# Rounding float64 weights with fewer VectorE instructions, and running the first tile's first two steps in parts

## The chip, the cores and the metric

One core of one Trainium2 chip. The metric is device time of one execution in microseconds (us). The kernel before takes 1192.2 us (median of 4 runs, 1190.4 to 1193.2).

Names: TensorE (PE in the profile) multiplies matrices, VectorE (DVE) and ScalarE (ACT) work elementwise, GpSimd (POOL) does the slow elementwise rest, and one queue (SPq) issues all the DMA requests of the program. The banks (bankA, mix and so on) are the pieces of memory that the matmuls write. A cold clock is a stretch in which the profile shows TensorE's granted clock at 0.50 of full speed.

## The reference, cut to what matters

```python
# B=8, H=8, S=576, D=64; x becomes (4608, 512); d_ff = 1536
scores = scale * q @ k.T                       # per batch and head
ret    = scores * gamma[h] ** (i - j)          # for i >= j, else 0
x      = (ret @ v) laid out as (B*S, H*D)
g      = x @ w_gate
out    = (silu(g) * (x @ w_val)) @ w_out       # w_* come as float64
```

## The kernel before

The attention runs in 32 "ticks" (batch and pair of heads). Each tick handles three stages of three neighbouring pairs: `values` of pair t-2, `scores` of pair t-1, `transposes` of pair t. The output is computed in nine tiles of 512 rows. The first tile is special: while it runs, the 18 blocks of weights (1 MB each, as 64-bit words) are loaded and turned into 32-bit floats by integer arithmetic. Later tiles use a scheme with fewer matmuls.

```python
def load_w(i):                     # three raw buffers; SP queue
    raw = rawp.tile([P, 1024], I64, tag="raw", bufs=RAWS)      # RAWS = 3
    nc.sync.dma_start(out=raw..., in_=src...)

def weight(i):                     # one block of weights
    nc.vector.tensor_scalar(out=ex, in0=hi, 20, 0x7FF, shift_right, and)
    nc.scalar.activation(out=ex, in_=ex, func=AF.Relu, bias=low, scale=float(1 << 23))
    nc.vector.tensor_scalar(out=man, in0=hi, 0xFFFFF, 0x100000, and, or)
    nc.vector.scalar_tensor_tensor(out=sig, in0=lo, 2.0 ** -32, in1=man, mult, add)
    nc.vector.scalar_tensor_tensor(out=ex, in0=hi, -(1 << 31), in1=ex, and, or)
    nc.vector.scalar_tensor_tensor(out=dst, in0=sig, 2.0 ** -20, in1=ex, mult, mult)
    load_w(the weight three further on)
...
def transposes(i):                 # of pair i
    ...; load(i + AHEAD)           # request the attention tiles of pair i + 2
    for hl in range(2):            # key scaling, on ScalarE
        nc.scalar.activation(out=kn[:, :, hl, :], in_=kn[:, :, hl, :], func=AF.Copy, scale=key[...])
...
def up(f):                         # one of 12 steps of the first tile
    ...16 matmuls into two banks...
    s = rawp.tile([P, TW], F32, tag="s", bufs=2)               # same pool as the raw weights
    nc.scalar.activation(out=s, in_=banks[0], func=AF.Silu)
    nc.vector.tensor_tensor(out=hs[:, f], in0=banks[1], in1=s, op=ALU.mult)
...
merge(ticks(0, 6), [weights 0, 1, 2])          # spread evenly, in program order
merge(ticks(6, 10), moe + four down groups)    # moe: 12 steps, 15 weights
first.close()                                  # the pool rawp is released here
up_ = tc.tile_pool(name="up", bufs=2)          # its tiles lie where rawp lay
xs[1] = combos_x(1)                            # sums for the second tile, VectorE
```

The program sets the order by hand: every engine runs its instructions in the order in which they are emitted.

## Time and profile before

| Part of the span | us | what bounds it |
|---|---|---|
| to 5 | 5 | first loads |
| 5 to 67.9 | 63 | loads, VectorE; the first two steps end at 67.9 |
| 67.9 to 208.9 | 141 | ten steps, four ticks, four down groups; TensorE with waits |
| 208.9 to 219.8 | 11 | the second tile's first two groups (3.5 us of matmuls) |
| 219.8 to 1190 | 970 | TensorE without idle time |

The prediction shows the lines it rests on. One more view: busy time by stretch of 30 us. The columns are stretch and length; busy us and number of instructions of PE, PEld (weight loads), DVE, ACT, POOL; granted TensorE clock; mean busy share of the 16 DMA engines (a value over 1 shows that it isn't exact); GB/s.

```profile
30.00:60.00 30.00, 23.38 (x223) 16.28 (x224) 24.87 (x44) 9.90 (x17) 0.00 (x0) 0.83 0.86 180
60.00:90.00 30.00, 30.00 (x133) 14.85 (x132) 25.23 (x36) 6.96 (x9) 3.87 (x2) 1.00 1.05 209
90.00:120.00 30.00, 21.68 (x110) 11.36 (x109) 28.06 (x38) 6.47 (x8) 1.26 (x1) 0.89 0.76 236
```

VectorE is at 24.9 to 28.1 of 30 us, and the DMA engines are nearly as full.

### The profile page before, as it was taken

The numbers are of one execution on the slowest core, as the hardware profiler recorded it, in microseconds if no ns is written. First come the engines' busy times: TensorE is split into PE (matmuls) and PEld (weight loads), VectorE is DVE, ScalarE is ACT, GpSimd is POOL, SyncE is SP. The second block draws the span as 40 slices with busy tenths as digits, with TensorE's granted clock in tenths as the row PEclk, the third lists the DMA queues.
The fourth block names the chain that finished last, engine by engine and source line by source line (L and its number), as shares of the span: only waits on it lengthen the run. The fifth ranks groups of instructions, "written<-read, shape, count | busy, mean of one in ns | idle before, by whom it ended". The sixth has DMA issues, their size and how long they took to land.

```text
span 1190.0 us, 16346 instructions
## 1 busy us (share of the span) xinstructions
PE 1149.8 (97%) x6660; PEld 945.7 (79%) x6660; DVE 519.3 (44%) x922; ACT 168.8 (14%) x324; POOL 425.8 (36%) x382
## 2 busy tenths in 40 slices
PE   5797999899999999999999999999999999999998
PEld 4543444688888888888888888888888888888887
DVE  3889940444335443444344444444343333333332
ACT  2322210111011110111011101110111001101110
POOL 0010100553433434444244325434344436345541
PEclk9898999899999999999999999999999999999999
DMA  9897610132212221222222221222000010000001
GB/s 233 182 212 226 205 34 32 22 66 40 40 36 45 53 49 47 40 40 39 66 49 39 40 57 42 55 40 48 28 1 1 1 36 1 1 18 18 1 0 36
DMA packets 228299, 65.96 MB, mean 55 GB/s; under 512 B 211584, under 2 KB 219776, under 8 KB 228224
## 3 DMA queue, kind: packets, MB, share of 16 engines
q1 hardware_dynamic: 228224, 64.92, 23.8%
q8 instruction: 52, 0.85, 0.3%
q14 instruction: 23, 0.19, 0.1%
HBM read 55.45 MB, written 9.44 MB: 55 GB/s over the span
## 4 chain that ended last, share of the span: by engine, by line
PE 89%; DVE 4%; SPq 3%; DMA 3%; issue 1%; ACT 0%; DVEq 0%; ACTq 0%
PE bankE L380 14%; PE bankC L380 14%; PE bankA L380 14%; PE bankB L380 7%; PE bankE L450 7%; PE bankC L450 7%; PE bankA L450 7%; PE bankB L450 3%; PE sc L264 2%; PE xo L286 2%; PE mix L270 1%; PE xo L294 1%; SPq L133 1%; PE bankA L338 1%; PE bankA L346 1%; PE bankE L338 1%
## 5 line engine op out<-in xcount | busy, mean ns | idle before, releaser
L380 PE MATMUL bankA<-x,w_up 128*128 128x256 f32 x768 | 182.0, 380 | 0.0
L424 POOL TENSOR_TENSOR hid<-c,ss 128x512 f32<-128x512 f32 x48 | 61.0, 1271 | 326.1 <-ACT ss L423 326.1
L380 PEld LDWEIGHTS bankA<-x,w_up 128*128 128x128 f32 x768 | 145.4, 190 | 20.4 <-issue 0.5
L380 PE MATMUL bankB<-t,s 128*128 128x256 f32 x384 | 92.6, 385 | 5.2 <-DVE t L369 5.2
L380 PE MATMUL bankE<-x,w_up 128*128 128x256 f32 x384 | 91.3, 381 | 0.0
L380 PE MATMUL bankE<-x,s 128*128 128x256 f32 x384 | 91.3, 381 | 0.0
L399 DVE TENSOR_TENSOR u<-bankB,u 128x512 f32<-128x512 f32 x48 | 33.2, 692 | 132.7 <-PE bankB L380 122.9
L380 PE MATMUL bankC<-t,s 128*128 128x256 f32 x384 | 91.1, 380 | 0.0
L380 PE MATMUL bankC<-t,w_up 128*128 128x256 f32 x384 | 90.7, 379 | 0.0
L380 PEld LDWEIGHTS bankB<-t,s 128*128 128x128 f32 x384 | 74.0, 193 | 15.8 <-POOL s L358 5.6
L450 PE MATMUL bankE<-w_dn,hid 128*128 128x256 f32 x384 | 86.1, 381 | 0.0
L450 PE MATMUL bankC<-t,hid 128*128 128x256 f32 x384 | 85.5, 379 | 0.0
L450 PE MATMUL bankA<-w_dn,hid 128*128 128x256 f32 x384 | 85.5, 379 | 0.0
L380 PEld LDWEIGHTS bankC<-t,s 128*128 128x128 f32 x384 | 73.4, 191 | 10.1
L380 PEld LDWEIGHTS bankC<-t,w_up 128*128 128x128 f32 x384 | 73.0, 190 | 9.9
L450 PEld LDWEIGHTS bankA<-w_dn,hid 128*128 128x128 f32 x384 | 73.0, 190 | 9.9
L450 PEld LDWEIGHTS bankC<-t,hid 128*128 128x128 f32 x384 | 73.0, 190 | 9.9
L380 PEld LDWEIGHTS bankE<-x,w_up 128*128 128x128 f32 x384 | 72.5, 190 | 10.0
L450 PEld LDWEIGHTS bankE<-w_dn,hid 128*128 128x128 f32 x384 | 72.5, 190 | 10.0
L380 PEld LDWEIGHTS bankE<-x,s 128*128 128x128 f32 x384 | 72.5, 190 | 10.0
L357 POOL TENSOR_TENSOR s<-w_up 128x512 f32<-128x512 f32 x48 | 61.4, 1279 | 51.4 <-DMA out_dram<-o 51.4
L415 ACT ACTIVATE s<-bankA 128x256 f32<-128x256 f32 x48 | 18.4, 383 | 353.0 <-PE bankA L380 353.0
(105 smaller groups left out, 1535.4 us busy)
## 6 DMA issues: line engine op xcount, KB each, us to landing
kn<-in_k_dram SPq DMA_DIRECT2D x64, 128.0 KB, 2.9
v<-in_v_dram SPq DMA_DIRECT2D x64, 128.0 KB, 3.0
qk<-in_q_dram SPq DMA_DIRECT2D x112, 72.0 KB, 2.5
qk<-in_k_dram SPq DMA_DIRECT2D x112, 72.0 KB, 2.6
raw<-in_moe_w_gate_dram SPq DMA_DIRECT2D x6, 1024.0 KB, 7.3
raw<-in_moe_w_val_dram SPq DMA_DIRECT2D x6, 1024.0 KB, 5.3
raw<-in_moe_w_out_dram SPq DMA_DIRECT2D x6, 1024.0 KB, 5.4
out_dram<-c SPq DMA_DIRECT2D x16, 256.0 KB, 2.2
```

Source lines behind the costliest of these rows:

```text
L133: nc.sync.dma_start(out=qk[a * SQ : (a + 1) * SQ, n], in_=src[b, 2 * p + a // 2, :, (a % 2) * SQ : (a % 2 + 1) * SQ].rearrange("(j t) d -> ...
L264: nc.tensor.matmul(sc[hl][:, ts(c, P)], kT[half[hl], ts(c, P)], qT[half[hl], ts(c, P)], start=True, stop=True)
L270: nc.tensor.matmul(z[half[hl], c], s["kn"][:, c, hl, :], s["v"][:, c, hl, :], start=True, stop=True)
L286: nc.tensor.matmul(xo[half[hl], ts(c, P)], s["v"][:, c, hl, :], ret[:, hl, ts(c, P)], start=(c == 0), stop=(c == 0), skip_group_check=True)
L294: nc.tensor.matmul(o[half[hl]], state[half[hl], c - 1, :], s["qT"][half[hl], c * P : c * P + w], start=False, stop=True, skip_group_check= ...
L338: nc.tensor.matmul(bank, w_up[:, u, gv, c // 2, c % 2, fb, :], x[:, c, :], start=(c == 0), stop=(c == HP - 1))
L357: nc.gpsimd.tensor_tensor(out=s2, in0=A(u, 1, 0), in1=A(u, 0, 0), op=ALU.subtract)
L380: nc.tensor.matmul(bank[:, gv * TH : (gv + 1) * TH], lhs(gv, c), rhs[:, c, :], start=(start and gv == 0 and c == 0), stop=(stop and c == 1 ...
L399: nc.vector.tensor_tensor(out=uu, in0=bankB, in1=uu, op=ALU.add)
L415: nc.scalar.activation(out=s, in_=bankA[:, 0:TH], func=AF.Silu)
L424: nc.gpsimd.tensor_tensor(out=hid[:, u, 1::2], in0=t["c"][:, :, 1], in1=s, op=ALU.mult)
L450: nc.tensor.matmul(bank[:, m * DH : (m + 1) * DH], lhs(u)[:, ts(m, P)], rhs(u), start=(start and u == 0 and m == 0), stop=(stop and u == N ...
```

## The change

The intent: VectorE's five instructions per weight become three, ScalarE splits the 64-bit words, TensorE is fed early by running steps 0 and 1 in parts as each quarter of `x` arrives, and the first tile's output buffers move out of the pool that is released. The diff, cut to its core:

```diff
+    io = ctx.enter_context(tc.tile_pool(name="io", bufs=2))
+    def split(i):
+        nc.scalar.activation(out=top, in_=high words as F32, func=AF.Copy, scale=2.0 ** -112)
+        nc.scalar.activation(out=ulp, in_=low words as U32, func=AF.Copy, scale=2.0 ** -29)
     def weight(i):
-        (five VectorE instructions and one ScalarE, above)
+        nc.vector.tensor_scalar(out=top, in0=top, scalar1=3, op0=ALU.logical_shift_left)
+        nc.vector.scalar_tensor_tensor(out=top, in0=hi, scalar=-(1 << 31), in1=top, and, or)
+        nc.vector.tensor_tensor(out=dst.bitcast(I32), in0=top, in1=ulp, op=ALU.add)
         load_w(order[k + RAWS])
+        split(order[k + 1])            # the next weight's split, right behind this weight
     load_w(0); load(1); load_w(1)
-    load_w(2)
 def transposes(i):
     load(i + AHEAD)
+    if i == 1: load_w(2)
-    key scaling of pair i on ScalarE
 def scores(i):
+    key scaling of pair i on ScalarE   # one tick later than before
-    s, o in rawp; ss in up_
+    s, o, ss in io
-    merge(ticks(0, done), [weights 0, 1, 2])
+    split(0)
+    for t in range(done):
+        tick(t)
+        if t in (1, 2, 3): weight(t - 1)
+        if 2 < t < 6: up(0 and 1, chunks 0 and 1 at t == 3, else chunk t - 2)
     moe: steps and weights, two weights ahead of step 2;
+    the last two weights both behind step 11
```

More of the change, by code (lines that the diff above doesn't have):

```diff
@@ L177 @@
     LEAD, RAWS = 3, 3
-    order = list(range(LEAD))
-    for f in range(2 * NU):
-        order += [LEAD + f] if LEAD + f < NUP else []
-        order += [NUP + f // 2] if f % 2 else []
+    behind = [[] for _ in range(2 * NU)]
+    for f in range(1, 2 * NU):
+        behind[f] += [LEAD + f] if LEAD + f < NUP else []
+        behind[f] += [NUP + (f - 3) // 2] if f % 2 and f > 1 else []
+    behind[1].insert(0, LEAD)
+    behind[-1].append(len(weights) - 1)
+    order = list(range(LEAD)) + sum(behind, [])
+    assert sorted(order) == list(range(len(weights)))
     first = ExitStack()
     rawp = first.enter_context(tc.tile_pool(name="rawp", bufs=1))
-    raws = {}
+    raws, parts = {}, {}
     def load_w(i):
@@ L190, in load_w @@
         raws[i] = raw.bitcast(I32).rearrange("p (n two) -> p n two", two=2)
-    def weight(i):
-        dst, bits = weights[i][1], raws.pop(i)
-        lo, hi = bits[:, :, 0].bitcast(U32), bits[:, :, 1]
-        ex = rawp.tile([P, 1024], I32, tag="ex", name="ex")
-        man = rawp.tile([P, 1024], I32, tag="man", name="man")
-        nc.vector.tensor_scalar(out=ex, in0=hi, scalar1=20, scalar2=0x7FF,
-                                op0=ALU.logical_shift_right, op1=ALU.bitwise_and)
-        nc.scalar.activation(out=ex, in_=ex, func=AF.Relu, bias=low, scale=float(1 << 23))
-        nc.vector.tensor_scalar(out=man, in0=hi, scalar1=0xFFFFF, scalar2=0x100000,
-                                op0=ALU.bitwise_and, op1=ALU.bitwise_or)
-        sig = man.bitcast(F32)
-        nc.vector.scalar_tensor_tensor(out=sig, in0=lo, scalar=2.0 ** -32, in1=man, op0=ALU.mult, op1=ALU.add)
-        nc.vector.scalar_tensor_tensor(out=ex, in0=hi, scalar=-(1 << 31), in1=ex,
-                                       op0=ALU.bitwise_and, op1=ALU.bitwise_or)
-        nc.vector.scalar_tensor_tensor(out=dst, in0=sig, scalar=2.0 ** -20, in1=ex.bitcast(F32),
-                                       op0=ALU.mult, op1=ALU.mult)
-        if order.index(i) + RAWS < len(order):
-            load_w(order[order.index(i) + RAWS])
@@ L213 @@
-    low = const.tile([P, 1], F32, name="low")
-    nc.gpsimd.memset(low, -896.0 * (1 << 23))
+    def split(i):
+        bits = raws[i]
+        top = rawp.tile([P, 1024], F32, tag="top", name="top", bufs=2)
+        nc.scalar.activation(out=top, in_=bits[:, :, 1].bitcast(F32), func=AF.Copy, scale=2.0 ** -112)
+        ulp = rawp.tile([P, 1024], I32, tag="ulp", name="ulp", bufs=2)
+        nc.scalar.activation(out=ulp, in_=bits[:, :, 0].bitcast(U32), func=AF.Copy, scale=2.0 ** -29)
+        parts[i] = top.bitcast(I32), ulp
@@ new lines, in weight @@
+    def weight(i):
+        dst, hi = weights[i][1], raws.pop(i)[:, :, 1]
+        top, ulp = parts.pop(i)
+        nc.vector.tensor_scalar(out=top, in0=top, scalar1=3, scalar2=None, op0=ALU.logical_shift_left)
+        nc.vector.scalar_tensor_tensor(out=top, in0=hi, scalar=-(1 << 31), in1=top,
+                                       op0=ALU.bitwise_and, op1=ALU.bitwise_or)
+        nc.vector.tensor_tensor(out=dst.bitcast(I32), in0=top, in1=ulp, op=ALU.add)
+        k = order.index(i)
+        if k + RAWS < len(order):
+            load_w(order[k + RAWS])
+        if k + 1 < len(order):
+            split(order[k + 1])
@@ L217 @@
         load(i)
-    for i in range(1, RAWS):
-        load_w(i)
+    load_w(1)
     kT = const.tile([P, S], F32, name="kT")
@@ L253, in transposes, with scores @@
             load(i + AHEAD)
+        if i == 1:
+            load_w(2)
+        st[i] = dict(qT=qT, kn=kn, v=vt, last=last)
+    def scores(i):
+        p, s = i % HP, st[i]
+        qT, kn = s["qT"], s["kn"]
         for hl in range(2):
@@ L256, in transposes @@
                                  scale=key[:, 2 * p + hl : 2 * p + hl + 1])
-        st[i] = dict(qT=qT, kn=kn, v=vt, last=last)
-    def scores(i):
-        p, s = i % HP, st[i]
-        qT = s["qT"]
         for c in range(NFULL):
@@ L269, in scores @@
             for hl in range(2):
-                nc.tensor.matmul(z[half[hl], c], s["kn"][:, c, hl, :], s["v"][:, c, hl, :], start=True, stop=True)
+                nc.tensor.matmul(z[half[hl], c], kn[:, c, hl, :], s["v"][:, c, hl, :], start=True, stop=True)
         for hl in range(2):
@@ L330, in plain, with up @@
         hs = hid.rearrange("p u b t -> p (u b t)").rearrange("p (f t) -> p f t", t=TW)
-        def up(f):
+        def up(f, chunks):
             u, fb = divmod(f, 2)
@@ L336, in up @@
             for gv, bank in enumerate(banks):
-                for c in range(HP):
+                for c in chunks:
                     nc.tensor.matmul(bank, w_up[:, u, gv, c // 2, c % 2, fb, :], x[:, c, :], start=(c == 0), stop=(c == HP - 1))
-            s = rawp.tile([P, TW], F32, tag="s", name="s", bufs=2)
-            nc.scalar.activation(out=s, in_=banks[0], func=AF.Silu)
-            nc.vector.tensor_tensor(out=hs[:, f], in0=banks[1], in1=s, op=ALU.mult)
+            if HP - 1 in chunks:
+                s = io.tile([P, TW], F32, tag="s", name="s")
+                nc.scalar.activation(out=s, in_=banks[0], func=AF.Silu)
+                nc.vector.tensor_tensor(out=hs[:, f], in0=banks[1], in1=s, op=ALU.mult)
         def down(i):
@@ L347, in down @@
                                  start=(f == 0), stop=(f == 2 * NU - 1))
-            o = rawp.tile([P, DM], F32, tag="s", name="o", bufs=2)
+            o = io.tile([P, DM], F32, tag="s", name="o")
             nc.scalar.copy(out=o, in_=bank)
             nc.sync.dma_start(out=out[n * TW + i * P : n * TW + (i + 1) * P, :], in_=o)
-        return [lambda f=f: up(f) for f in range(2 * NU)] + [lambda i=i: down(i) for i in range(TW // P)]
+        return up, down
     def combos_up(u):
@@ L421, in p4 @@
                                     in1=t["u"].rearrange("p g t -> p (g t)"), op=ALU.add)
-            s = up_.tile([P, 2, TH], F32, tag="ss", name="ss", bufs=1)
+            s = io.tile([P, 2, TH], F32, tag="s", name="ss")
             nc.scalar.activation(out=s, in_=t["c"][:, :, 0], func=AF.Silu)
@@ L510, in p2 @@
             mm(bankA, h(1), w(1, 0), False, True)
-            s = up_.tile([P, 2, DH], F32, tag="ss", name="ss", bufs=1)
+            s = io.tile([P, 2, DH], F32, tag="s", name="o")
             nc.scalar.copy(out=flat(s), in_=bankA)
@@ L547 @@
     done = needed(0)
-    merge(ticks(0, done), [lambda i=i: weight(i) for i in range(LEAD)])
-    steps = plain(0)
-    moe = []
-    for f in range(2 * NU):
-        moe += [lambda i=LEAD + f: weight(i)] if LEAD + f < NUP else []
-        moe.append(steps[f])
-        moe += [lambda u=f // 2: weight(NUP + u)] if f % 2 else []
-    merge(ticks(done, needed(1)), moe + steps[2 * NU :])
+    up, down_plain = plain(0)
+    split(0)
+    for t in range(done):
+        tick(t)
+        if t in (1, 2, 3):
+            weight(t - 1)
+        if t - 2 in range(HP) and t > 2:
+            for f in range(2):
+                up(f, range(2) if t == 3 else [t - 2])
+    moe = []
+    for f in range(1, 2 * NU):
+        moe += [lambda f=f: up(f, range(HP))] if f > 1 else []
+        moe += [lambda i=i: weight(i) for i in behind[f]]
+    merge(ticks(done, needed(1)), moe + [lambda i=i: down_plain(i) for i in range(TW // P)])
     done = needed(1)
```

## The prediction

> **What bounds the kernel now.** I read the page first: its busy shares, then its 40 slices.
>
> ```profile
> PE 1149.8 (97%) x6660; PEld 945.7 (79%) x6660; DVE 519.3 (44%) x922; ACT 168.8 (14%) x324; POOL 425.8 (36%) x382
> PE   5797999899999999999999999999999999999998
> DVE  3889940444335443444344444444343333333332
> ```
>
> TensorE bounds the whole, and from slice 8 (about 220 us) on it has no idle time to give. The change can only shorten the opening, the first tile; there VectorE is at 8 to 9 tenths in slices 1 to 4. So the question is how much TensorE idles before 220 us. The waits of TensorE in the first 330 us answer it (engine, line, whom it waited for: us, times, longest):
>
> ```profile
> PE mix L267 <- DVE x L309: 18.7, 5, 8.3
> PE bankA L244 <- DMA qk<-in_q_dram: 8.1, 2, 5.3
> PE bankB L380 <- DVE t L369: 5.2, 1, 5.2
> PE bankB L244 <- DMA kn<-in_k_dram: 2.1, 3, 1.0
> ```
>
> The 18.7 us are five waits for one small VectorE instruction that frees a PSUM bank. The timeline shows why it is late: it stands in VectorE's queue behind a weight conversion (start, duration, instruction):
>
> ```profile
> 161.02 0.69 DVE L341 TENSOR_TENSOR hid<-bankE,s 128x512 f32<-128x512 f32 x1 [6.18 <-PE bankE L338]
> 161.63 0.68 DVE L199 TENSOR_SCALAR ex<-raw 128x1024 int32<-128x1024 int32 x1
> ...
> 166.49 0.22 DVE L309 TENSOR_TENSOR x<-mix,tab 128x64 f32<-128x64 f32 x1
> ```
>
> The chain that ended last shows the 5.2 us at the end of the first tile:
>
> ```profile
> 209.19 0.59 ACT o L349
> 209.80 2.00 DMA out_dram<-o
> 211.92 0.70 DVE t L367
> 212.65 1.64 DVE x L368
> 214.32 1.64 DVE t L369
> 216.05 3.75 PE bankB L380 x8
> 219.80 2.04 PE bankC L380 x8
> ```
>
> The second tile's sums wait for the last store of the first tile, because their buffers lie where the released pool with `o` lay. Then the eight matmuls take 3.75 us; later groups of the same kind take 1.73.
>
> The conversion's cost by instruction (count, busy us, mean ns):
>
> ```profile
> L205 DVE SCALAR_TENSOR_TENSOR man<-raw,man 128x1024 f32<-128x1024 uint32 x18 | 22.2, 1232 | 0.6
> L206 DVE SCALAR_TENSOR_TENSOR ex<-raw,ex 128x1024 int32<-128x1024 int32 x18 | 21.9, 1217 | 0.6 <-ACT ex L201 0.6
> L202 DVE TENSOR_SCALAR man<-raw 128x1024 int32<-128x1024 int32 x18 | 13.4, 746 | 0.0
> L199 DVE TENSOR_SCALAR ex<-raw 128x1024 int32<-128x1024 int32 x18 | 12.7, 705 | 16.3 <-DMA raw<-in_moe_w_gate_dram 14.0 <-DMA raw<-in_moe_w_out_dram 1.5 <-DMA raw<-in_moe_w_val_dram 0.7
> L201 ACT ACTIVATE ex<-ex,low 128x1024 int32<-128x1024 int32 x18 | 20.7, 1150 | 77.4 <-DVE ex L199 77.4
> DMA to landing us min/median/max: 4.8/5.5/8.6
> ```
>
> The last line is for the raw weights, 1 MB each. The fifth conversion instruction (L208) has a mean of 1308 ns into `w_up`.
>
> **What the Trainium skill says.** "VectorE: DVE Perf Modes", the perf-mode tier table: an fp32 one-source operation from SBUF runs at two elements a cycle, a tensor_tensor at one. The trace agrees for these 32-bit words: about 0.7 us against 1.22 for 1024. The same page's Specifications say integer operands are converted to fp32 and exact only below 2^24; if so, the new integer addition rounds the weights a little, which costs no time; no run yet shows it. "ScalarE: Activation LUTs", What ACT_TABLE_LOAD costs: 186 ns + 0.833 ns an element with immediates, 93 more for a pointer operand. For 1024 that is 1132 ns with the bias of before (trace: 1150) and 1039 without. "TensorE: Matmul & The Clock Gate", Part 1: after about 3.4 us of idling the array runs at half rate for a similar time. The trace agrees: after a wait of 3.8 us at 50 us, eight matmuls into bankA took 6.06 us instead of 3.43.
>
> **The change part by part.**
> VectorE: five instructions become three. One shift (0.69), one sign merge (1.22), one add of two SBUF tensors (1.22): 3.13 us, against 0.69+0.69+1.23+1.22+1.23 = 5.06. 18 x 1.93 = 35 us less VectorE work.
> ScalarE: one activation of 1.15 becomes two of about 1.04, so 18 x 0.93 = 17 us more. It is 20 to 33% busy in the opening, so the load is harmless. The position isn't: each engine keeps program order, and the split of weight k+1 stands right after weight k. It then blocks whatever follows on ScalarE until that raw weight has landed. I see three places.
> (a) The first split precedes tick 0. Weight 0 landed at 14.0 us (the first VectorE instruction started then), so the copies of qT, which ran at 6.5, run at 16.0. TensorE's first scores move from 9.2 to about 17.3. Before, tick 1 then waited to 15.5 for its load anyhow, so tick 1 ends near 23.7 and little is lost against before.
> (b) Weight 2 is now requested behind the fourth attention load, which can't start before tick 1's transposes (23.7) and takes 6.8 us to issue. 23.7 + 6.8 + 5.5 = 36. Its split ends at 38, the key scaling of tick 3 at 39; TensorE is ready at 33.6. About 6 us idle, and a cold clock after.
> (c) Weight 6 is requested behind the load of tick 5 (14 issues, 7.6 us, after VectorE's transposes). Its split stands ahead of tick 6's key scaling: about 4 us idle.
>
> TensorE, traced forward by these durations: tick 2 ends at 30; tick 3 with (b) at 42; the first part of the two moved steps (8 half-banks, 6.9 us, 1.5 for the cold clock) at 50.5; tick 4 at 54.8; 3.4 us of parts, 58.2; tick 5 at 62.4; the last 3.4 us of parts, 65.8. Before, the same work (bankE of the second step) ended at 67.9. So moving the two steps, 13.7 us of matmuls, into the gaps gains about 2 us, because the new ScalarE waits take up the gaps.
> From there TensorE must run ten steps of two banks of 3.43, so 6.87 each, 68.7; four ticks of 4.1 (67.9 to 71.9 in the timeline), 16.4; four down groups of 10.3, 41.2; two groups of the second tile, 3.5: together 129.8.
> Gaps on top: waiting for weight 3 0.6; tick 6 0.9 + 4.3 and 1.5 cold; tick 7 0.8; tick 8 about 0; tick 9: weights 16 and 17 now both stand between the last product and the bank's release, 0.7 + 6.26 + 0.2 against 3.2 us of other TensorE work, 4.0, and 1.5 cold. Sum 13.6.
> The wait at the end of the tile goes: the output tiles now lie in a pool of their own, so the sums run during the down groups, 41 us earlier. That takes out 5.2 and the cold 2.0.
> So the second group of the second tile ends at 65.8 + 129.8 + 13.6 = 209.2 instead of 219.8: 10.6 us less, 1182. Of this 7.2 are the end of the tile, 2 the moved steps, the rest smaller waits behind shorter conversions. After 220 us nothing changes but one more buffer for `ss`, whose engine has slack.
>
> **The rivals.**
> First, a clean win: if no ScalarE wait appears, TensorE runs on from tick 2 at 23.7: 8 ticks of 4.1, 2 transposes of 1.8, 24 banks of 3.43, 41.2 and 3.5 give 32.8+3.6+82.3+41.2+3.5+23.7 = 187 instead of 219.8; 1160. For it: VectorE's 35 us are real work on a busy engine. Against: the program order on ScalarE, and the order of requests.
> Second, DMA becomes the bound. Its share was 0.91, 0.86 and 1.05 in the first three stretches of 30 us, and up to the last weight it moves some 31 MB at about 230 GB/s, 135 us. The last weights are needed near 150, so it just fits; but three raw buffers cover only two landings ahead, and each late one now also blocks Silu and key scaling. That would give back 5 to 10 us more: 1187 to 1192.
> Third, the tile's end alone matters and all else cancels: 1185.
>
> **Range and chances.** The step sum says 1182. Gaps of hand-traced queues can fall together, so I lean a little towards the win: 1180.5, with 1169 to 1189 as the range. Faster by over 2% needs under 1168.8, more than twice my gain and most of the clean win: 0.11. Slower by over 2% would need a new wait in the long part, which I see nowhere: 0.01.
>
> **What would show it.** Right: VectorE's conversion in three groups of about 0.69, 1.22, 1.22 us; ScalarE idle until 14 us for the first raw weight; TensorE's matmuls of `mix` from `kn` waiting for ScalarE in ticks 3 and 6; no wait of L369's kind before the second tile; the first down group starting near 164.5 instead of 167.7. Wrong: TensorE without waits from 24 us on (the clean win), Silu held by raw weights in many steps (DMA), a conversion over 4 us, or a change after the first tile.

## The result, and the profile after

The changed kernel takes 1184.07 us (median of 4 runs, 1183.73 to 1184.24), 0.9933 of the kernel before (95% interval 0.9916 to 0.995): 8 us less.

The page first: VectorE has 36 us less work (519.3 before), ScalarE 18 us more (168.8), and TensorE is as dense as before from slice 8 on.

```profile
PE 1145.0 (97%) x6660; PEld 942.2 (80%) x6660; DVE 483.5 (41%) x886; ACT 186.7 (16%) x342; POOL 422.7 (36%) x381
```

The new conversion, groups on VectorE and then on ScalarE (count, busy us, mean ns):

```profile
L215 DVE SCALAR_TENSOR_TENSOR top<-raw,top 128x1024 int32<-128x1024 int32 x18 | 22.1, 1225 | 0.6
L217 DVE CUSTOM_DVE_ANT_0 w_up<-top,ulp 128x2048 uint16<-128x2048 uint16 x12 | 14.7, 1225 | 0.8
L214 DVE TENSOR_SCALAR top<-top 128x1024 int32<-128x1024 int32 x18 | 12.3, 682 | 0.0
...
L203 ACT ACTIVATE top<-raw 128x1024 f32<-128x1024 f32 x18 | 20.7, 1148 | 48.3 <-DMA raw<-in_moe_w_gate_dram 27.9 <-DVE w_up L217 12.4 <-DMA raw<-in_moe_w_out_dram 5.0
```

The integer addition turns up as a custom instruction on 16-bit halves; it takes 1.225 us all the same. The last line is the one that matters: ScalarE stood 48.3 us idle at the head of a split, mostly for raw weights that had not landed.

Whom TensorE waited for, in the first 330 us (compare the list in the prediction):

```profile
PE mix L280 <- ACT kn L270: 11.3, 2, 6.0
PE sc L274 <- ACT kT L253: 8.1, 1, 8.1
PE mix L277 <- DVE x L319: 6.7, 4, 4.2
PE bankA L252 <- DMA qk<-in_q_dram: 5.2, 1, 5.2
...
```

The wait for the bank fell from 18.7 to 6.7 us, and the one of 5.2 us at the tile's end is gone. Two came: 11.3 us for the scaled keys, which is new, and 8.1 us for the first copies (0.5 before), both on ScalarE. The chain of waits shows how the larger one comes about:

```profile
73.97 5.47 DMA raw<-in_moe_w_gate_dram
79.52 1.12 ACT top L203
80.64 1.01 ACT ulp L205
82.09 1.51 PE mix L280 x16
83.60 5.28 PE bankC L348 x8
...
208.59 1.73 PE bankA L391 x8
210.32 1.73 PE bankB L391 x8
```

Weight 6 is requested at 74.0, although its raw buffer was free from 66.6: the 14 requests of the load of pair 7 stood ahead of it in the queue, from 66.2 to 73.9. It lands at 79.5, is split until 81.5, then the keys of tick 6 are scaled, and only then can TensorE go on. Then a cold clock stretches eight matmuls from 3.43 to 5.28 us (the mean granted clock of the stretch from 60 to 90 us is 0.89). At the end, the second tile's second group follows the first without a gap and ends at 212.05 (210.32 + 1.73) instead of 219.80. That difference, 7.75 us, is nearly the whole gain: the span is 8.0 us shorter. The second tile's sums now run during the down groups; the last of them on VectorE:

```profile
169.81 0.69 DVE L380 TENSOR_TENSOR t<-x 128x512 f32<-128x512 f32 x1
```

After the second group nothing changed: from the start of the third to the end are 970.4 us before and 970.1 after, so the second buffer for `ss`, which came with the new pool, is no rival.

### The profile page after: what moved, and what is told of

The parts are those of the page before. It is cut to its first block, busy times and chain, and to the rows that moved or that the text cites. A ratio compares the mean times of both kernels' runs of the same rounds, so it can differ in the third digit from the quotient of the medians.

```text
span 1182.0 us, 16354 instructions
## 1 busy us (share of the span) xinstructions
PE 1145.0 (97%) x6660; PEld 942.2 (80%) x6660; DVE 483.5 (41%) x886; ACT 186.7 (16%) x342; POOL 422.7 (36%) x381
## 4 chain that ended last, share of the span: by engine, by line
PE 95%; DMA 1%; DVE 1%; ACT 1%; SPq 1%; issue 1%; DVEq 0%; ACTq 0%
PE bankE L391 14%; PE bankA L391 14%; PE bankC L391 14%; PE bankE L461 7%; PE bankC L461 7%; PE bankB L391 7%; PE bankA L461 7%; PE bankB L461 4%; PE sc L274 3%; PE xo L296 2%; PE bankC L348 2%; PE mix L280 2%; PE bankB L348 2%; PE bankA L348 2%; PE xo L304 2%; PE bankE L348 1%
## 5 line engine op out<-in xcount | busy, mean ns | idle before, releaser
L461 PE MATMUL bankC<-t,hid 128*128 128x256 f32 x384 | 85.5, 379 | 0.0
L461 PE MATMUL bankA<-w_dn,hid 128*128 128x256 f32 x384 | 85.5, 379 | 0.0
```

What stands on the lines that cost most here:

```text
L461: nc.tensor.matmul(bank[:, m * DH : (m + 1) * DH], lhs(u)[:, ts(m, P)], rhs(u), start=(start and u == 0 and m == 0), stop=(stop and u == N ...
```

## The experiments

The theory to test: the gain is the end of the first tile; all else cancels, since ScalarE's stands at late weights take back what the shorter conversion gives. The rivals: the conversion itself pays; the parts pay; DMA is the bound. Twelve kernels ran, all with results that agree with the reference within its tolerance. Runs of one call shared a chip and its runs of the kernel before (median 1192.1, 1193.5, 1192.5 and 1192.8 us in the four calls), so runs of different calls are compared by their ratios.

| run | what | median us | ratio to before | 95% interval |
|---|---|---|---|---|
| changed kernel | all | 1184.1 | 0.9933 | 0.9916 to 0.995 |
| e1 | before + pool | 1186.1 | 0.9947 | 0.9934 to 0.9959 |
| e2 | changed - pool | 1192.2 | 0.9996 | 0.9984 to 1.0009 |
| e3 | changed, steps whole | 1184.6 | 0.9935 | 0.9923 to 0.9948 |
| e4 | changed, keys early | 1178.1 | 0.9882 | 0.9867 to 0.9897 |
| e5 | changed, tick 9 first | 1178.2 | 0.9871 | 0.9856 to 0.9886 |
| e6 | changed, first split later | 1184.3 | 0.9922 | 0.9909 to 0.9935 |
| e7 | before + conversion | 1189.7 | 0.9961 | 0.9948 to 0.9975 |
| e8 | before + conversion + pool | 1182.3 | 0.9903 | 0.9889 to 0.9917 |
| e9 | changed, split in place | 1177.7 | 0.9878 | 0.9863 to 0.9893 |
| e10 | changed, loads later | 1175.7 | 0.9854 | 0.9835 to 0.9872 |
| e11 | e9 + e5 | 1172.8 | 0.9836 | 0.9824 to 0.9848 |
| e12 | e11 + loads later | 1166.6 | 0.9775 | 0.9758 to 0.9792 |

### The pool alone, and all but the pool (e1, e2)

```diff
 # e1, on the kernel before          # e2 is the reverse, on the changed kernel
+    io = tc.tile_pool(name="io", bufs=2)
-    s, o = rawp.tile(...); ss = up_.tile(...)
+    s, o, ss = io.tile(...)
```

> The kernel before with only the separate pool for the output tiles (no new conversion, no moved steps). Theory (the end of the first tile is worth 7.2 us of the 8, the rest of the change nearly cancels): about 1185, within 2 us of the changed kernel. Rival (the shorter conversion is what pays, the pool only a little): above 1189.

> The changed kernel with the output tiles back in the released pool. Theory: the wait for the last store before the second tile's sums is back, 7 us more than the changed kernel: about 1191, the same as before within 2 us. Rival: within 2 us of the changed kernel (1184), because the end of the tile is hidden by something else now.

Both as the theory had it. The pool alone gives 0.53%, 6.3 us; without it the rest of the change gives nothing that can be told from zero (0.9996). The trace of the changed kernel without the pool has the old wait back, to the tenth:

```profile
PE mix L279 <- ACT kn L269: 11.5, 2, 6.1
...
PE bankB L390 <- DVE t L379: 5.2, 1, 5.2
```

The traces agree more closely than the times. From the start of the second tile's first group to the start of its third are 10.7 us before and in e2, 3.5 in the changed kernel and in e1: 7.2 us. The rest of the difference (6.3 and 8) lies in the opening, where the four begin the second tile at 208.9, 209.3, 208.4 and 210.3 us.

### The first two steps whole (e3)

```diff
-        if t - 2 in range(HP) and t > 2:
-            for f in range(2): up(f, range(2) if t == 3 else [t - 2])
+    for f in range(2): up(f, range(HP))       # after tick 5
```

> The changed kernel with the first two steps run whole after tick 5 instead of in parts. Theory (the parts fill little: without them ticks 4 and 5 end earlier by nearly what the parts took, as the loads allow it): 0 to 2 us slower than the changed kernel, 1184 to 1186. Rival (the parts fill true gaps): 5 us or more slower, 1189 or above.

It runs within 0.5 us of the changed kernel. The trace says why: without the parts, tick 4 starts at once, and the two steps follow in one piece. Their last bank, and the next step:

```profile
61.14 3.60 PE L348 MATMUL bankE<-x,w_up 128*128 128x512 f32 x8
64.58 3.60 PE L348 MATMUL bankA<-x,w_up 128*128 128x512 f32 x8
```

The next step starts at 64.6; with the parts it starts at 63.8. So the parts are worth 0.8 us in the trace, and nothing that the times can tell.

### The keys a tick earlier (e4)

```diff
 def transposes(i):
+    key scaling of pair i on ScalarE          # as before the change
 def scores(i):
-    key scaling of pair i on ScalarE
```

> The changed kernel with the key scaling back where it was before, a tick earlier, ahead of the weight splits. Theory (TensorE's waits of 5.3 and 6.0 us in ticks 3 and 6 are ScalarE standing at a split whose weight has not landed): both waits of TensorE for the scaled keys go, with the cold clock after them about 9 us: 1174 to 1177. Rival (the waits are the load of the attention tiles or the banks, ScalarE is only named last): within 2 us of 1184.

1178.1, 6 us faster, where the theory had 7 to 10. (The profiled execution was the slowest of the five, 1181.3.) The waits for keys are gone, so ScalarE's order caused them. But its other work stands behind the same splits, and the wait comes back elsewhere:

```profile
PE mix L277 <- DVE x L319: 11.9, 4, 5.9
...
PE bankA L348 <- ACT qT L253: 4.4, 1, 4.4
```

In tick 3 the copies of the next pair are now late (4.4), and in tick 7 the bank's release (5.9), behind weight 8.

### The last tick ahead of the last weights (e5)

```diff
-    ... step 11, weight 16, weight 17, tick 9, down groups
+    ... step 11, tick 9, weight 16, weight 17, down groups
```

> The changed kernel with tick 9 ahead of the last two weights instead of behind them. Theory (the 4.2 us wait for the bank's release and about 2 us of cold clock come from the two conversions in front of it; the down group needs the last weight only near its end): 5 to 6 us faster than the changed kernel, 1178 to 1179. Rival (the wait turns into one for the last weight inside the first down group): within 1.5 us of 1184.

1178.2, as the theory had it. The longest wait for the bank fell from 4.2 to 1.1 us, and the first down group waits 0.6 us for the last weight, near its end.

### The first split behind tick 0 (e6)

```diff
-    split(0)
     for t in range(done):
         tick(t)
+        if t == 0: split(0)
```

> The changed kernel with the split of the first weight behind tick 0, so that ScalarE's copies of tick 0 no longer wait to 16 us. Theory (the 8 us idle at the start cost nothing, since the fourth load and weight 2 are requested at the same time either way, and tick 3 waits for those): within 1 us of the changed kernel, 1183 to 1185. Rival (8 us of TensorE idling is a loss): 4 us or more faster, 1180 or below.

1184.3: no difference, as expected. TensorE starts its scores at 9.2 us instead of 17.0, and then waits longer in ticks 1 and 3:

```profile
16.55 1.51 PE L280 MATMUL mix<-v,kn 128*64 128x64 f32 x16 [4.90 <-ACT kn L270]
...
38.02 1.51 PE L280 MATMUL mix<-v,kn 128*64 128x64 f32 x16 [7.16 <-ACT kn L270]
```

Tick 3 waits for weight 2, which was requested at 30.0 us here and at 29.4 in the changed kernel. An idle time of 8 us that stands ahead of such a wait costs nothing. This run also corrects a reason in the prediction: the fourth load did not start at 23 us because of tick 1's transposes, which ended at 20 here while the load started at 23 all the same, but because the requests ahead of it kept the queue busy until then.

### The conversion alone, and with the pool (e7, e8)

```diff
 # e7, on the kernel before; keys, requests, steps and pools untouched
-    five VectorE instructions, one ScalarE
+    split(next weight) on ScalarE, three VectorE instructions
 # e8: and the pool of e1
```

> The kernel before with only the new conversion, each weight's split one weight ahead; key scaling, order of requests, steps and pools as before. Theory (the shorter conversion is worth much where VectorE was late, and the new order gives most of it back by ScalarE's waits): the waits of 8.3, 1.6, 2.7 and 3.8 us for the bank's release shrink, 10 to 15 us faster than before: 1178 to 1182. Rival (the conversion is off the path or the splits block ScalarE here too): within 4 us of before, 1188 or above.

> The kernel before with the new conversion and the separate pool for the output tiles, nothing else. Theory: the two gains lie one after the other and add up, 7 us below the run with the conversion alone: 1171 to 1175, faster than the changed kernel by some 10 us. Rival (they overlap): no better than 1182.

The conversion alone gives 0.39%, 4.6 us, not 10 to 15: here the theory's size was wrong, and the result lies in the rival's range. I had put the old waits for the bank down to VectorE's long instructions alone. With short ones, the four fall from 16.4 to 7.1 us in all (8.3 to 4.1, 3.8 to 2.1, 2.7 to 1.0, 1.6 to none), but a new one of 4.4 comes in tick 6. It and the one of 4.1 in tick 7 have the same root: VectorE waits for a Silu, which stands on ScalarE behind a split, which waits for its raw weight.

```profile
72.10 0.48 PE L271 MATMUL mix<-qT,kT 64*64 64x64 f32 x4 [4.44 <-DVE x L313]
...
103.15 0.33 PE L271 MATMUL mix<-qT,kT 64*64 64x64 f32 x4 [4.08 <-DVE x L313]
```

With the pool it is 1182.3. The two gains add up (0.53% and 0.39%, together 0.97%), as expected, though from the smaller base: the range of 1171 to 1175 stood on e7's forecast and was missed with it. On the same chip e6, which equals the changed kernel, has 1184.3. So the two simple parts of the change, in the old order, are some 2 us better than the whole; the intervals overlap a little, so what is safe to say is that no gain of the new order and the parts shows.

### The split in its own place (e9), and with the last tick moved (e11)

```diff
 def weight(i):
+    split(i)                                  # right ahead of its own VectorE work
     ...
-    split(order[k + 1])
```

> The changed kernel with each weight's split on ScalarE right ahead of its own three VectorE instructions in program order, instead of right behind the weight before; nothing else moved. Theory (what costs TensorE is other ScalarE work standing behind a split whose weight has not landed, not the landing itself): the waits of 5.3 and 6.0 us for scaled keys in ticks 3 and 6 and their cold clock go and no other wait of that size takes their place: 1173 to 1177. Rival (the weights arrive too late in any order, as in the run with the conversion alone and the one with the early keys, where a wait for the bank's release of 4 to 6 us took its place): 1178 to 1184.

> The run before this one with tick 9 ahead of the last two weights as well. Theory: the two waits lie one after the other, so the gain of 5.9 us of the tick's move adds to that of the split's place: 1167 to 1171, faster than the kernel before by 2% or nearly. Rival (the gains overlap, the last weight arrives late): 1174 or above.

1177.7 and 1172.8. Both lie between the theory's range and the rival's, and the trace shows that "no other wait of that size takes their place" was wrong. The waits for keys are gone, but in tick 7 TensorE waits for VectorE, which waits for weight 8:

```profile
102.92 0.48 PE L276 MATMUL mix<-qT,kT 64*64 64x64 f32 x4 [8.09 <-DVE x L318]
```

That is from e11. Weight 8 was requested at 92.9 us, behind the 14 requests of the load of pair 8, which took from 78.7 to 92.8; its raw buffer was free from 85.5. So a second cause stood behind the first: the order of requests in the one queue.

### The attention loads later (e10, e12)

```diff
 def transposes(i):
-    load(i + 2)
+    load(i + 2) unless i in (5, 6, 7, 8)
     ... weight 4;  + load(7)   ... weight 7; + load(8)
     ... weight 9;  + load(9)   ... weight 15; + load(10)
```

> The changed kernel with four attention loads (those of ticks 7 to 10) requested two to five weights later, so that the weights stand ahead of them in the one queue of requests; ScalarE's order untouched. Theory (weight 6 landed at 79.5 us only because its request stood behind the load of tick 7; ScalarE's stand at the split follows from that): TensorE's wait for keys in tick 6 (6.0 us and 2.6 us of cold clock) goes, the one in tick 3 (5.3) stays, and no wait of more than 2 us takes its place before tick 9: 1175 to 1178. Rival (the DMA engines are at their rate in this stretch, so any order only moves the wait): 1181 to 1185.

> The run with the splits in place and tick 9 ahead of the last weights, with the same four attention loads requested later. Theory: its remaining wait of 8.1 us in tick 7 (weight 8 behind the load of tick 8, landed at 98 us) and the 2 us of cold clock after it go: 1162 to 1166, 2% or more below the kernel before. Rival (rate of the DMA engines): 1170 to 1173, no better than without it.

(The loads moved by two or three weights, not up to five.) On the changed kernel this alone gives 1175.7, the theory's range: 8.4 us less by the medians, 9.4 by the ratios, with ScalarE's order untouched. Weight 6 is now requested at 66.9 instead of 74.0 us and is there at 72.1. In tick 6 nobody waits for keys any more:

```profile
75.84 0.33 PE L277 MATMUL mix<-qT,kT 64*64 64x64 f32 x4 [0.95 <-DVE x L319]
76.10 0.69 PE L280 MATMUL mix<-v,kn 128*64 128x64 f32 x16
76.71 3.70 PE L348 MATMUL bankC<-x,w_up 128*128 128x512 f32 x8
```

So in the changed kernel the rate of the DMA engines was not the bound here; the same bytes in another order removed the wait. All three corrections together give 1166.6, 0.9775 of the kernel before and the fastest of all, a little above the range (1162 to 1166). What stays in tick 7 is a wait of 3.0 us (8.1 in e11), and there the DMA engines are nearly full. The stretches of e12:

```profile
60.00:90.00 30.00, 28.53 (x129) 14.01 (x129) 21.10 (x31) 11.89 (x15) 2.58 (x2) 1.00 1.00 255
90.00:120.00 30.00, 27.02 (x120) 13.84 (x120) 22.79 (x33) 14.71 (x19) 1.28 (x1) 0.89 0.96 228
```

Shares of 1.00 and 0.96 for 60 us, against 0.77 and 0.67 in the changed kernel. But an order of requests is in it too: VectorE's work there begins with weight 7, requested at 81.4 behind the load of pair 7, whose 14 requests took 13.1 us. Which of the two is the bound, and whether still fewer waits can be had by order alone, stays open.

## Why the prediction was right

It said 1180.5 (step sum 1182), within 2%; the result is 1184.07. It was right in outcome: the end of the tile gave 7.2 us, just as predicted. Of the other 3.4 us that it forecast, for the opening, 0.5 came (the second tile begins at 208.4 us instead of 208.9), so the result is nearest to its third rival, the end of the tile alone, 1185. Most steps were right in place, not all in size:

| step | predicted | measured |
|---|---|---|
| conversion on VectorE | 0.69, 1.22, 1.22 | 0.68, 1.225, 1.225 |
| one split activation | 1.04 | 1.15 |
| (a) first scores | 17.3 | 17.0 |
| (b) wait for keys in tick 3 | about 6 | 5.3 |
| last parts end | 65.8 | 63.8 |
| (c) wait for keys in tick 6 | 4.3 | 6.0 |
| cold clock after (c) | 1.5 | 2.6 |
| weight 3; tick 6, 7, 8 for the bank | 0.6; 0.9, 0.8, 0 | 0.5; 1.0, 0.95, 0 |
| tick 9 for the bank, cold clock after | 4.0, 1.5 | 4.2, 2.3 |
| first down group starts | 164.5 | 165.5 |
| second tile's second group ends | 209.2 | 212.05 |

- The end of the tile, "7.2 are the end of the tile": right, 7.2 in the traces. In the times the pool alone is worth 6.3 us, and taking it out of the changed kernel costs 8.
- ScalarE's three stands at a split were right in place. (a) cost nothing, as said, and e6 shows it. The reason given for the time in (b) was wrong (e6), its number right by luck. (c) was 1.7 us too small.
- The gaps' sum was mis-sized: 13.6 predicted; measured 0.5 + 1.0 + 6.0 + 2.6 + 0.95 + 4.2 + 2.3 = 17.5. Of the 3.9 us missing, 1.9 are cold clock, 1.7 are (c). The start was 2.0 us better than I had it. Together they make 211.1 out of 209.2; the last 1 us to 212.05 is undisturbed work, 129.8 us by the sum and about 130.7 measured. That the two errors partly cancel is luck.
- The cold clock was mis-sized by the prediction's own line: 6.06 us instead of 3.43 is a loss of 2.6, not 1.5. There the granted clock stood at 0.50 from about 49.7 to 56.5 us, twice the "similar time" of 3.4 that the prediction says the trace agrees with.
- "Moving the two steps gains about 2 us": not borne out. Run whole, they cost 0.8 us in the trace and 0.5 us in the medians, inside the noise.
- "The rest smaller waits behind shorter conversions", 1.4 us by the sum: the conversion alone is worth 4.6 us in the old order (e7), and in the new order nothing is left of it beside the pool (e2 against before).
- The lean from 1182 towards 1180.5 was in the wrong direction. It was hedging, not argument. (2% below 1192.2 is 1168.4, not 1168.8; nothing hangs on it.)
- The rival that DMA becomes the bound was half right: late weights are what ScalarE and VectorE stand for, but e10 shows that the order of requests made them late, not the rate. The clean win of 1160 is nearly what e12 reaches (1166.6) by taking most of the waits away.

## What to carry to other kernels

When work moves from a busy engine to an idle one, look at where it stands in that engine's program order: an instruction that waits for a transfer holds up everything behind it, and this idle engine fed the critical one. When transfers share one queue, request what is needed first, first; a load that isn't due for two stages can hide the one that is. And look for pool releases before touching arithmetic: the buffer that moved to another pool was worth 6 to 7 of the 8 us, and 35 us less work on a busy engine gave 4.6 alone.

## What the Trainium skill lacked or had wrong

- "VectorE: DVE Perf Modes", Specifications, has integer operands exact only below 2^24. The integer addition here isn't a tensor_tensor on int32 in the trace: it is a custom instruction on 2048 16-bit halves, 1.225 us for 1024 words, as long as an fp32 pass. The page doesn't mention this form, and no other page has it. Whether it is exact above 2^24 no run shows; all results passed the comparison.
- "ScalarE: Activation LUTs", What ACT_TABLE_LOAD costs: the 1039 ns worked out for immediates (an estimate from its figures) are 10% under the measured 1148 ns (36 instructions). The form with a bias operand, worked out as 1132, measured 1150. So the 93 ns between the two forms don't show here; but the new form reads every second 32-bit word and the old one a dense tile, which no run separates. In a pair the second starts 1.01 to 1.07 us after the first, so the records overlap by about 0.1 us (the section gives 93 ns) and the predicted 1.04 was right as a spacing.
- "TensorE: Matmul & The Clock Gate", Part 1, has half rate after an idle window of about 3.4 us, and then for the first 3.4 us or so of work; that would cost about 1.7 us (an estimate from its figure). Against mix and bank groups at full clock (3.43 us for eight matmuls), TensorE lost 3.1 us after a wait of 3.8 (before, at 50 us), 2.3 and 2.6 after 4.2 and 6.0 (changed), 2.6 after 8.1 (e11), but only 1.6 after 8.3 (before, at 104 us): mostly more than 1.7, and not in step with the wait. Read in stretches of 0.25 us, the clock stood at 0.50 for 6.8 us each of these times, in e11 for 10.2, two or three times the 3.4; part of it passed in the wait, and the loss is about half of what TensorE worked in the rest (3.4 us of work in the case of 1.6). The clock also fell with waits shorter than the page's window: 3.0 us (e12, 2.8 lost) and 2.1 us (e7, 1.8 lost, 3.4 us at 0.50), though not with one of 2.7 (before, at 167 us).
- "SBUF — State Buffer", Who interferes with whom, has a VectorE instruction with two SBUF inputs contend with GpSimd. The traces fit this and give the size: two of the second tile's sums took 1.63 us each beside GpSimd in the kernel before, and 0.69 us in the changed kernel, where GpSimd was idle. No run changes that alone.
- "DMA: Bandwidth & Descriptors", Issuing engines are not separate DMA queues, calls the time to initiate a DMA usually small against the DMA itself. Here the 14 requests of one attention load took 7.6 us to issue, about 0.5 us each, against 2.5 to 3.0 us from issue to landing, and 14 us when the DMA engines were full (e11).
